# Moving half of a projection ahead of the last head's gather, and adding four strips in vector rows instead of a matrix product

## The chip, the cores and the metric

The kernel runs on one core of one Trainium2 chip. The metric is the device time of one execution in microseconds (us). Executions of one kernel agree to one or two tenths of a per cent (the six runs of before span 0.11%). All runs quoted were of the fast state. A ratio is the mean time of one kernel's fast runs over that of the other's of the same rounds, so it is not quite the ratio of the medians that are quoted.

In the profile, PE is TensorE's matmuls, PEld its weight loads, DVE is VectorE, ACT is ScalarE, SP the engine that issues the loads and stores. L733 is a line of the kernel's text; the changed kernels have other line numbers for the same code.

## The reference

Two attention blocks for one token: a large one, A (32 heads, 32,768 keys each), and a small one, B (32 query heads over 8 key heads, the last 4,096 keys). Each ends in a projection with its own `wo`.

```python
q = (x @ wq) per head
p = softmax(q @ k.T * Dh**-0.5)           # Dh = 128; B only over its last 4096 keys
o = p @ v                                  # 32 heads x 128
a = o_A.reshape(1, 32*128) @ wo_A          # [1, 512]
b = o_B.reshape(1, 32*128) @ wo_B          # [1, 512]
return concatenate([a, b], axis=-1)        # [1, 1, 1024], bf16
```

## The kernel before

The kernel streams keys and values of A head by head: TensorE transposes keys, VectorE copies the transposes out, TensorE forms scores and the value product. At the end of a head VectorE combines four diagonal blocks of the value product ("the combine") into `oc`, and TensorE puts the result into its row of a table G ("the gather"). After the last head G is normalised and spread over partitions, and the two projections follow.

```python
# end of emit_PV, the last step of each head
pv = self.emit_gather(name, g, DH, DH + 1)      # the softmax sum's column
for j in range(4):                               # VectorE: combine the four diagonal blocks
    ...
self.accread = o
self.gath = self.emit_gather(name, g, 0, DH)     # TensorE: the 128 values; waits for the combine
```

```python
def emit_proj(self):
    top = self.WO_CUTS["A"][1]                   # WO_CUTS: A (0,11,19,25,29,31,32), B (0,16,32)
    for part in range(len(self.WO_CUTS["B"]) - 1):        # small projection, four row strips of S
        o = self.proj_part("B", part, lambda e, lhsT, rhs, a: e.matmul(
            self.S[32 * (a % 4):32 * (a % 4) + 1, :], ..., tile_position=(0, 32 * (a % 4)), ...))
    strips = self.op("dve", ... tensor_copy(self.pb[:, :], self.S[:, :]), o)
    rows = o = self.op("pe", ... matmul(self.ACC[0:1, :], lhsT=self.e32[:, 0:1], rhs=self.pb[:, :]), strips, ...)
    o = self.op("dve", ... tensor_copy(self.qrow[0:1, :], self.ACC[0:1, :]), o)
    self.op("sp", ... dma_start(self.out[0, :, 512:1024], self.qrow[0:1, :]), o)
    row = self.proj_part("A", 0, ... self.T[1][0:1, :] ...)          # large projection, piece 1: 11 matmuls
    row = self.op("dve", ... tensor_copy(self.pb[0:1, :], self.T[1][0:1, :]), row, rows)  # "the T-row copy"
    for part in range(1, len(self.WO_CUTS["A"]) - 1):                # pieces 2 to 5, halves in PT
        if part == 3:
            self.op("pe", ... add the T-row to PT with a 1x1 matmul, row)
        self.proj_part("A", part, ...)
    ...                                          # piece 6, output copies, store
```

Each piece of a projection waits for its own load of `wo`. Each operation raises **one** semaphore, that of one reading engine (`to`). A second reading engine is kept in `pending`, and gets its signal from a **later** operation of the same engine that has a free signal:

```python
for o in ops:                                    # in assign(), for each engine's operations in order
    ...
    if to is None:
        to = next((c for c in users + pending), None)   # users: the engines that read this operation
    o.to = to
    pending = [c for c in dict.fromkeys(pending + users) if c != to]
```

That is correct as long as an engine's later operation ends after its earlier one, as in the trace of before (TensorE's small projection ends at 1312.92, the strip product at 1314.73, the first large piece at 1317.11), and every run here was correct. It says nothing about when. Engines are taken in the order PE, DVE, ACT, POOL, SP.

## Time and profile before

| | us |
|---|---|
| median of the first 3 runs (range) | 1323.32 (1322.72 to 1324.0) |
| span of the profiled run | 1321.7 |
| last data of `wo` landed (semaphore record in the trace) | 1318.82 |
| last matmul ends | 1320.02 |

From the page: the DMA row gives the busy share of the 16 DMA engines in 40 slices, in tenths.

```profile
DMA  9999999999999999999999999999999999999998
...
DMA packets 13359, 570.59 MB, mean 432 GB/s; under 512 B 1570, under 2 KB 1700, under 8 KB 2084
```

The load stream is full from end to end. The timeline of TensorE, in the middle of the loop and at the start of the last head (columns: start us, us, engine, line, operation, what it writes <- reads, count, and in brackets the idle time before it and what ended that):

```profile
661.72 3.49 PE L553 MATMUL psT<-ident,kbuf 128*128 128x128 bf16 x31 [4.82 <-DMA kbuf<-in_A_k_cache_dram]
...
1275.77 1.40 PE L553 MATMUL psT<-ident,kbuf 128*128 128x128 bf16 x22 [0.95 <-PEq L262]
```

In the middle of the loop TensorE waits 4.8 us for keys. In the last head, whose keys are there already, it waits only for its own sequencer at the end of the loop turn. The chain of waits at the end (start us, us, what):

```profile
1309.67 3.27 PE psS L733 x32
...
1312.97 0.70 DVE pb L736
...
1313.71 1.02 PE psACC L737 x2
1314.73 2.27 PE psT L741 x11
1317.01 3.02 PE psPT L719 x42
...
1320.05 0.41 DVE out_sb L726
```

The chain holds no load: the small projection (L733), strip copy, strip product (L737) and large projection (L741, L719) follow each other, and the last matmul ends 1.2 us after the last landing. The last view has busy time by stretches (us and instructions for each engine, then PEclk, the granted clock); the stretches are those on which the clock was granted:

```profile
core 0: us, PE busy (x) PEld busy (x) DVE busy (x) ACT busy (x) POOL busy (x), PEclk, DMA share, GB/s
1305.68:1309.09 3.41, 1.28 (x20) 0.54 (x12) 1.83 (x6) 0.00 (x0) 0.00 (x0) 1.00 0.99 421
1309.09:1312.50 3.41, 3.10 (x32) 1.11 (x36) 0.26 (x2) 0.00 (x0) 0.00 (x0) 0.50 0.98 415
1312.50:1315.90 3.40, 2.60 (x17) 0.70 (x10) 1.37 (x2) 0.00 (x0) 0.00 (x0) 1.00 1.00 419
```

The small projection fell into a stretch at half clock, the large one into stretches at full clock.

### The profile page before, as it was taken

Reading aid. Unit: us, or ns where it says so; the run is one execution under the profiler, and the core shown is the slowest. Engines: PE = TensorE matmul, PEld = TensorE weight load, DVE = VectorE, ACT = ScalarE, POOL = GpSimd, SP = SyncE. Lnnn points to the kernel's source line nnn. Section 1 sums busy time; section 2 is a strip of 40 time slices with the busy share of each in tenths; the row PEclk is TensorE's granted clock in tenths of the full one; section 3 lists DMA queues with packets and bytes.
Section 4 is the critical chain, followed back from the end, with each engine's and each line's share of the span. In section 5 each row is a group of like instructions: output and inputs, shape, how many; then the busy total and the mean of one; then the engine's idle time right before and its main releaser. Section 6 shows DMA issues by size and latency. Waiting matters only on the chain. (4 is left out here: it accounts for less than half of the span.)

```text
span 1321.7 us, 28783 instructions
## 1 busy us (share of the span) xinstructions
PE 968.2 (73%) x13243; PEld 673.7 (51%) x13243; DVE 750.7 (57%) x1341; ACT 55.1 (4%) x168; POOL 2.6 (0%) x22
## 2 busy tenths in 40 slices
PE   4675768777677878767787777678777667877787
PEld 3353446555444655544465544446554445555453
DVE  3563556664555666455566645556665456665563
ACT  0000000000000000000000000000000000000000
POOL 0000000000000000000000000000000000000000
PEclk9886788887878888787888878888887788888788
DMA  9999999999999999999999999999999999999998
GB/s 404 434 434 431 440 434 434 434 436 432 433 436 436 428 438 434 428 438 434 428 442 430 428 442 432 430 438 434 437 432 432 438 430 434 438 428 436 436 428 365
DMA packets 13359, 570.59 MB, mean 432 GB/s; under 512 B 1570, under 2 KB 1700, under 8 KB 2084
## 3 DMA queue, kind: packets, MB, share of 16 engines
q1 hardware_dynamic: 13060, 570.43, 99.8%
q8 instruction: 8, 0.13, 0.0%
q10 hardware_dynamic: 288, 0.00, 0.0%
q14 instruction: 3, 0.02, 0.0%
HBM read 570.43 MB, written 0.00 MB: 432 GB/s over the span
## 5 line engine op out<-in xcount | busy, mean ns | idle before, releaser
L557 DVE COPY kt<-psT 128x1024 bf16<-128x1024 bf16 x1056 | 654.3, 683 | 236.9 <-PE psT L553 235.5
L553 PE MATMUL psT<-ident,kbuf 128*128 128x128 bf16 x8448 | 577.8, 234 | 169.0 <-DMA kbuf<-in_A_k_cache_dram 154.4
L553 PEld LDWEIGHTS psT<-ident,kbuf 128*128 128x128 bf16 x8448 | 538.1, 106 | 261.2 <-DMA kbuf<-in_A_k_cache_dram 162.5
L656 PE MATMUL psACC<-vbuf,ptsb 128*4 128x512 bf16 (+1 forms) x2112 | 187.0, 531 | 22.8 <-ACT ptsb L631 22.0
L576 PE MATMUL psS<-kt,qw 128*32 128x512 bf16 x2048 | 157.7, 385 | 14.9 <-DVE kt L557 14.9
L670 DVE TENSOR_SCALAR oc_A<-psACC,hot_A 128x128 f32<-128x128 f32 x32 | 11.2, 350 | 251.9 <-PE psG L683 251.9
L656 PEld LDWEIGHTS psACC<-vbuf,ptsb 128*4 128x4 bf16 (+1 forms) x2112 | 59.8, 111 | 140.4 <-issue 93.1
L604 ACT ACTIVATE psb<-psS,nb_A 128x512 bf16<-128x512 f32 x32 | 22.0, 687 | 1166.5 <-DVE nb_A L603 1166.5
L576 PEld LDWEIGHTS psS<-kt,qw 128*32 128x32 bf16 x2048 | 34.0, 95 | 57.6 <-DVE kt L557 30.8
L683 PE MATMUL psG<-oc_A,hw 128*32 128x128 f32 (+1 forms) x128 | 19.3, 227 | 52.3 <-DVE oc_A L672 52.3
L683 PEld LDWEIGHTS psG<-oc_A,hw 128*32 128x32 f32 x128 | 11.4, 109 | 62.4 <-DVE oc_A L672 55.0
L628 PE MATMUL psPT<-ident,psb 128*128 128x128 bf16 x136 | 18.3, 279 | 34.0 <-ACT psb L604 34.0
L672 DVE SCALAR_TENSOR_TENSOR oc_A<-psACC,hot_A,oc_A 128x128 f32<-128x128 f32 x96 | 33.6, 350 | 3.4
L593 DVE TENSOR_REDUCE tr_in<-psS 128x1 f32<-128x512 f32 x34 | 23.5, 692 | 17.2 <-PE psS L576 17.2
L628 PEld LDWEIGHTS psPT<-ident,psb 128*128 128x128 bf16 x136 | 10.3, 119 | 37.1 <-ACT psb L604 36.7
L597 PE MATMUL psACC<-rows,tr_in 128*1 128x64 f32 x64 | 8.7, 217 | 25.6 <-DVE tr_in L593 25.6
L631 ACT ACTIVATE ptsb<-psPT 128x512 bf16<-128x512 bf16 x34 | 20.3, 597 | 30.9 <-PE psPT L628 30.9
L597 PEld LDWEIGHTS psACC<-rows,tr_in 128*1 128x1 f32 x64 | 2.7, 81 | 35.1 <-DVE tr_in L593 35.1
L601 PE MATMUL psACC<-mr_A,nscale 1*128 1x1 f32 x64 | 12.1, 256 | 9.8 <-DVE mr_A L600 9.8
L601 PEld LDWEIGHTS psACC<-mr_A,nscale 1*128 1x128 f32 x64 | 9.4, 182 | 15.8 <-DVE mr_A L600 15.8
L603 DVE COPY nb_A<-psACC 128x1 f32<-128x1 f32 x32 | 5.0, 157 | 15.1 <-PE psACC L601 15.1
L600 DVE TENSOR_REDUCE mr_A<-psACC 1x1 f32<-1x64 f32 x32 | 6.8, 213 | 11.7 <-PE psACC L597 11.7
(82 smaller groups left out, 74.9 us busy)
## 6 DMA issues: line engine op xcount, KB each, us to landing
kbuf<-in_A_k_cache_dram SPq DMA_DIRECT2D x4, 4096.0 KB, 23.2
kbuf<-in_B_k_cache_dram SPq DMA_DIRECT2D x2, 4096.0 KB, 31.6
vbuf<-in_B_v_cache_dram SPq DMA_DIRECT2D x2, 4096.0 KB, 25.4
vbuf<-in_B_wq_dram SPq DMA_DIRECT2D x1, 4096.0 KB, 12.4
vbuf<-in_A_wq_dram SPq DMA_DIRECT2D x1, 4096.0 KB, 31.9
kbuf<-in_B_wo_dram SPq DMA_DIRECT2D x2, 2048.0 KB, 33.1
kbuf<-in_A_wo_dram SPq DMA_DIRECT2D x1, 1408.0 KB, 27.4
kbuf<-in_A_wo_dram SPq DMA_DIRECT2D x1, 1024.0 KB, 29.5
```

Source lines behind the costliest of these rows:

```text
L553: inst = e.transpose(T[:, 128 * k:128 * k + 128], src[:, DH * k:DH * k + DH], self.ident[:, :])
L557: self.copies.append(self.op("dve", lambda v: v.tensor_copy(KT[:, :], T[:, :]), o, to="pe"))
L576: inst = e.matmul(self.S[32 * c:32 * c + 32, :], lhsT=win, rhs=self.kt[(bb + c // 2) % NKT][:, 512 * (c % 2):512 * (c % 2) + 512], start=b ...
L593: o = dve(lambda v: v.reduce_max(tr["in"][:, 0:1], self.S[:, :], axis=AXX), self.sdone, self.k_pool, to="pe" if name == "A" else None)
L597: o = self.op("pe", lambda e: e.matmul(self.ACC[0:1, 0:64], lhsT=tr["in"][:, 0:1], rhs=self.rows64[:, :], start=True, stop=True, skip_grou ...
L601: o = self.op("pe", lambda e: e.matmul(self.ACC[:, 64:65], lhsT=self.nscale[:, :], rhs=t["mr"][0:1, :], start=True, stop=True, skip_group_ ...
L604: self.sread = self.op("act", lambda s: s.activation(out=self.psb[:, :], in_=self.S[:, :], func=ACTF.Exp, bias=t["nb"][:, k:k + 1], scale= ...
L628: inst = e.transpose(PT[:, 128 * jj:128 * jj + 128], self.psb[:, 128 * jj:128 * jj + 128], self.ident[:, :])
L631: self.ptread = self.op("act", lambda s: s.activation(out=self.ptsb[:, :], in_=PT[:, 0:512], func=ACTF.Copy), self.psread, to="pe")
L656: inst = e.matmul(acc[32 * c:32 * c + rows, 0:512], lhsT=lhsT, rhs=rhs, start=begin, stop=end, tile_position=(0, 32 * c), skip_group_check ...
L672: o = self.op("dve", lambda v, src=src, hot=hot: v.scalar_tensor_tensor(out=oc, in0=src, scalar=hot, in1=oc, op0=ALU.mult, op1=ALU.add), p ...
L683: return self.op("pe", lambda e: e.matmul(self.G[0:32, c0 + c:c0 + c2], lhsT=win, rhs=t["oc"][g % len(t["oc"])][:, c:c2], start=False, sto ...
```

## The change

The intent is to shorten TensorE's tail. Half of the small projection is put ahead of the last head's gather, to run while VectorE combines. For that the gather of each head moves to the start of the next loop turn, and the last one stands after the loop. The four strips are added in rows on one partition by ScalarE (two copies) and VectorE (one copy, three adds), so the strip copy and the fp32 product leave TensorE's path. A few clears are moved or added.

```diff
@@ the loop and what follows it
             self.emit_qcopy(g)
+            self.gath = self.emit_gather("A", g - 1, 0, DH)
             self.emit_unit("A", g)
 ...
+        self.emit_proj_b(0)
+        self.gath = self.emit_gather("A", NQH - 1, 0, DH)
         self.emit_spread("A")
         self.emit_proj()
@@ end of emit_PV
-        self.gath = self.emit_gather(name, g, 0, DH)
+        if name == "B":
+            self.gath = self.emit_gather(name, g, 0, DH)
@@
+    def sum_strips(self, o):
+        S = [self.S[32 * c:32 * c + 1, :] for c in range(STRIPS)]
+        row = [self.kt[c][0:1, :].bitcast(F32) for c in range(STRIPS)]
+        act = lambda c: self.op("act", lambda e: e.activation(out=row[c], in_=S[c], func=ACTF.Copy), o)
+        add = lambda out, a, b, *deps: dve(lambda v: v.tensor_tensor(out=out, in0=a, in1=b, op=ALU.add), *deps)
+        one, three = act(1), act(3)
+        two = dve(lambda v: v.tensor_copy(row[2], S[2]), o)
+        x = add(row[0], S[0], row[1], o, one)
+        y = add(row[2], row[2], row[3], two, three)
+        return add(self.qrow[0:1, :], row[0], row[2], x, y)
@@ emit_proj
-        for part in range(len(self.WO_CUTS["B"]) - 1):
-            o = self.proj_part("B", part, ...)
-        strips = self.op("dve", ... tensor_copy(self.pb[:, :], self.S[:, :]), o)
-        rows = o = self.op("pe", ... matmul(self.ACC[0:1, :], lhsT=self.e32[:, 0:1], rhs=self.pb[:, :], ...), strips, ...)
-        o = self.op("dve", ... tensor_copy(self.qrow[0:1, :], self.ACC[0:1, :]), o)
+        o = self.emit_proj_b(1)
+        o = self.sum_strips(o)
 (cut: the clears, the zero gather of the first turn, pb cut to one row)
```

More of the change, by code (lines that the diff above doesn't have):

```diff
@@ L284, in alloc @@
         self.m4 = sb("m4", [1, 128], F32)
-        self.pb = sb("pb", [128, 512], F32)
+        self.pb = sb("pb", [1, 512], F32)
         self.out_sb = sb("out_sb", [1, 512], BF16)
@@ L456, in constants @@
             pattern=[[-32, 4], [-1, 16]], compare_op=ALU.is_equal, fill=0.0, base=0, channel_multiplier=1), rows)
+        pool(lambda g: g.memset(c["A"]["oc"][0][:, :], 0.0))
+        self.k_hw = pool(lambda g: g.memset(self.hw[:, :], 0.0))
         pool(lambda g: g.memset(self.nscale[:, :], -self.SCALE))
@@ L460, in constants @@
             self.k_pool = pool(lambda g, n=n: g.memset(c[n]["b"][:, :], 0.0))
-        self.k_hw = pool(lambda g: g.memset(self.hw[:, :], 0.0))
         dve = lambda fn, *deps, **k: self.op("dve", fn, *deps, **k)
@@ L684, in emit_gather @@
             self.G[0:32, c0 + c:c0 + c2], lhsT=win, rhs=t["oc"][g % len(t["oc"])][:, c:c2], start=False, stop=True,
-            skip_group_check=True), self.accread, self.sread, self.hcopy if name == "A" else self.k_sel, to="dve")
+            skip_group_check=True), *(self.accread, self.sread, self.hcopy if name == "A" else self.k_sel) if g >= 0 else
+            (self.k_hw, self.accread), to="dve")
     def emit_spread(self, name):
@@ L727, in store, with emit_proj_b @@
         return self.op("act", lambda e: e.activation(out=out, in_=src, func=ACTF.Copy), dep)
+    def emit_proj_b(self, part):
+        return self.proj_part("B", part, lambda e, lhsT, rhs, a: e.matmul(
+            self.S[32 * (a % 4):32 * (a % 4) + 1, :], lhsT=lhsT, rhs=rhs, start=(a < 4), stop=(a >= 28),
+            tile_position=(0, 32 * (a % 4)), skip_group_check=True))
+    def sum_strips(self, o):
+        S = [self.S[32 * c:32 * c + 1, :] for c in range(STRIPS)]
+        row = [self.kt[c][0:1, :].bitcast(F32) for c in range(STRIPS)]
+        dve = lambda fn, *deps: self.op("dve", fn, *deps)
+        act = lambda c: self.op("act", lambda e: e.activation(out=row[c], in_=S[c], func=ACTF.Copy), o)
[5 more added lines that the diff above has]
+        return add(self.qrow[0:1, :], row[0], row[2], x, y)
     def emit_proj(self):
         top = self.WO_CUTS["A"][1]
-        for part in range(len(self.WO_CUTS["B"]) - 1):
-            o = self.proj_part("B", part, lambda e, lhsT, rhs, a: e.matmul(
-                self.S[32 * (a % 4):32 * (a % 4) + 1, :], lhsT=lhsT, rhs=rhs, start=(a < 4), stop=(a >= 28),
-                tile_position=(0, 32 * (a % 4)), skip_group_check=True))
-        strips = self.op("dve", lambda v: v.tensor_copy(self.pb[:, :], self.S[:, :]), o)
-        rows = o = self.op("pe", lambda e: e.matmul(self.ACC[0:1, :], lhsT=self.e32[:, 0:1], rhs=self.pb[:, :], start=True,
-                                             stop=True, skip_group_check=True), strips, self.accread)
-        o = self.op("dve", lambda v: v.tensor_copy(self.qrow[0:1, :], self.ACC[0:1, :]), o)
+        o = self.emit_proj_b(1)
+        o = self.sum_strips(o)
         self.op("sp", lambda e: e.dma_start(self.out[0, :, 512:1024], self.qrow[0:1, :]).then_inc(self.outsem["B"], 16), o)
@@ L742, in emit_proj @@
             self.T[1][0:1, :], lhsT=lhsT, rhs=rhs, start=(a == 0), stop=(a == top - 1), skip_group_check=True))
-        row = self.op("dve", lambda v: v.tensor_copy(self.pb[0:1, :], self.T[1][0:1, :]), row, rows)
+        row = self.op("dve", lambda v: v.tensor_copy(self.pb[:, :], self.T[1][0:1, :]), row)
         for part in range(1, len(self.WO_CUTS["A"]) - 1):
             if part == 3:
-                self.op("pe", lambda e: self.halves(e, self.PT, self.e32[0:1, 0:1], self.pb[0:1, :], False, False), row)
+                self.op("pe", lambda e: self.halves(e, self.PT, self.e32[0:1, 0:1], self.pb[:, :], False, False), row)
             self.proj_part("A", part, lambda e, lhsT, rhs, a: self.halves(e, self.PT, lhsT, rhs, a == top, False)
```

## The prediction

> **What bounds the kernel now.** The load stream. The page's DMA row shows 9 tenths in all but the last slice: 570.59 MB at 432 GB/s. In the trace's packets the stream starts 2 us into the span, has no pause, and its last data packet ends near 1318.3 of 1321.7 us. In the loop the timeline shows TensorE 4.8 us idle per head (at 661.72, for instance) until keys land, while each value load is issued some 8 us before the key load ahead of it is through. [...] So nothing that TensorE saves inside the loop can count; only the tail can.
>
> **The tail before** (timeline, chain of waits). The last value product ends about 1306.35; VectorE combine 1306.62 to 1308.14; gather 0.42; normalise and spread to 1309.6; small projection 3.27 (32 matmuls); strip copy on VectorE 0.70; fp32 strip product 1.02 (TensorE stands 0.74 for the copy, about 0.86 for the product); the large projection, 1314.6 to 1320.03, back to back; out copies 0.41; store. The large block's six wo pieces have landed (semaphore records) at 1312.28, 1314.75, 1316.65, 1317.87, 1318.48, 1318.82. TensorE is 1.2 us behind the loads at the end.
>
> **What the change does.**
> - In each loop turn the gather moves past the loop branch, so the 0.95 us of sequencer time before the transposes (at 1275.77 a wait on PEq) runs under VectorE's 1.5 us combine. 31 turns have this swallowed by the wait for keys; only the last head, which starts without waiting for a load, keeps it: about 0.9 us.
> - Half of the small projection (1.65 us) goes under the last combine. The loop exit now stands ahead of it, so about 0.8 us is real.
> - Strip copy and product leave TensorE: 1.6 us. In their place two ScalarE rows, one VectorE copy and three VectorE adds, about 0.68 us each (estimate from 1x512 copies at 0.679 and 128x512 ScalarE copies at 0.60 to 0.69): some 2.8 us instead of 2.5 to the small result, off the path; VectorE is free before the T-row copy is wanted.
> - A gather of zeros in the first turn, a small memset: nothing.
>
> Sum on TensorE: about 3.3 us. But it then meets the loads. After the last landing, 1318.82, 4 short matmuls remain (0.3 to 0.4 us), against an end at 1320.03 now. So I expect 0.8 to 0.9 us of the 3.3 in the time; the rest becomes TensorE waiting for wo pieces.
>
> **Prediction: 1322.5 us**, 1321.0 to 1324.2 for 8 in 10 (the three runs before spread over 1.3 us, more than the gain). Faster by over 2%: 0.4%; within 2%: 99%; slower: 0.6%.
>
> **What would show it.** Loop: same 432 GB/s, waits for keys about 0.9 us longer per head. Last head's transposes about 0.9 us earlier. Tail: 16 small matmuls between the last value product and the gather; TensorE waits for wo before the large pieces; last matmul ending 0.3 to 0.4 us after the last landing; the chain of waits ending in a DMA landing.
>
> **What would make it wrong.** The granted clock flips between 0.5 and 1.0 in steps of 3.41 us (0.5 from 1309.09 to 1312.5). With more waiting in the tail, 0.5 could be granted during the large projection; 11 matmuls of 0.21 us would take 0.43 and the tail end up to 2 us later than now (I give 10%). [...] Or the sum on VectorE delays the T-row copy.

0.9, 0.8 and 1.6 us make the 3.3 us on TensorE, of which 0.8 to 0.9 us were expected in the time.

## The result, and the profile after

Measured: 1325.45 us median (1325.02 to 1327.86, 6 runs), against 1322.84 (1322.54 to 1324.0, 6 runs) for before in the same comparison. The ratio is 1.0023, with a 95% interval of 1.001 to 1.0036: a small loss, clear of noise, where a small gain had been predicted. The measured median lies above the predicted range.

The page of the kernel after, the same lines:

```profile
DMA  9999999999999999999999999999999999999997
...
DMA packets 13360, 570.59 MB, mean 431 GB/s; under 512 B 1571, under 2 KB 1701, under 8 KB 2085
```

The stream is the same, and so are the landings: the last data of `wo` had landed at 1318.89 (1318.82 before). The timeline answers the two lines shown of before, and adds the two halves of the small projection:

```profile
661.77 3.49 PE L557 MATMUL psT<-ident,kbuf 128*128 128x128 bf16 x31 [4.81 <-DMA kbuf<-in_A_k_cache_dram]
...
1274.81 2.41 PE L557 MATMUL psT<-ident,kbuf 128*128 128x128 bf16 x40
...
1304.36 1.03 PE L737 MATMUL psS<-kbuf,oz_B 128*1 128x512 bf16 x13
...
1309.06 1.85 PE L737 MATMUL psS<-kbuf,oz_B 128*1 128x512 bf16 x16 [1.62 <-DMA kbuf<-in_B_wo_dram]
```

The loop is unchanged, the last head starts 0.96 us earlier, and half of the small projection does run ahead of the gather. TensorE now waits for loads already at the small block's second piece. So far this is the plan. The chain of waits shows what came after:

```profile
1312.41 4.17 PE psT L760 x11
1316.58 1.00 PE psPT L725 x10
...
1317.60 0.60 ACT kt L746
...
1318.22 0.69 DVE kt L747
...
1318.91 0.69 DVE kt L747
...
1319.63 0.68 DVE qrow L747
1320.31 0.61 DVE pb L762
...
1320.96 1.46 PE psPT L725 x17
...
1322.45 0.41 DVE out_sb L732
```

It reads as follows. The small projection was done near 1310.9. ScalarE copies its first strip (`kt L746`) only at 1317.60, at once after TensorE's work on `psPT`, which belongs to the *large* projection. VectorE's three adds follow, then the T-row copy (`pb L762`), and only then can TensorE add the T-row and finish. The waits (engine, line and what it waited for: us in total, times, longest) say the same:

```profile
ACT kt L746 <- PE psPT L725: 18.5, 1, 18.5
...
DVE kt L747 <- ACT kt L746: 6.6, 1, 6.6
...
PE psPT L725 <- DVE pb L762: 2.8, 1, 2.8
```

The stretches by granted clock show a second difference: the first piece of the large projection (L760, 11 matmuls) ran mostly at half clock: 4.17 us on the chain of waits, where before took 2.27 us at full clock.

```profile
1305.71:1309.13 3.42, 0.74 (x10) 0.37 (x14) 1.04 (x4) 0.00 (x0) 0.00 (x0) 1.00 1.00 428
1309.13:1312.54 3.41, 1.90 (x17) 0.41 (x18) 0.69 (x1) 0.00 (x0) 0.00 (x0) 0.50 0.97 413
1312.54:1315.96 3.42, 3.42 (x10) 1.01 (x9) 0.00 (x0) 0.00 (x0) 0.00 (x0) 0.50 0.99 413
```

### The profile page after: what moved, and what is told of

Read it like the earlier page. It is cut to its first block, busy times and chain, and to the rows that moved or that the text cites. A ratio compares the mean times of both kernels' runs of the same rounds, so it can differ in the third digit from the quotient of the medians.

```text
span 1324.1 us, 28790 instructions
## 1 busy us (share of the span) xinstructions
PE 969.3 (73%) x13243; PEld 674.8 (51%) x13243; DVE 752.5 (57%) x1343; ACT 56.4 (4%) x170; POOL 2.8 (0%) x23
## 4 chain that ended last, share of the span: by engine, by line
DMA 70%; PE 28%; DVE 2%; issue 0%; ACT 0%; SPq 0%
DMA kbuf<-in_A_k_cache_dram 65%; PE psT L557 23%; PE psS L580 4%; DMA kbuf<-in_B_k_cache_dram 3%; DMA kbuf<-in_A_wo_dram 2%; DVE kt L561 1%; PE psACC L660 0%; PE psT L760 0%; PE psPT L725 0%; DVE kt L747 0%; DVE oc_A L676 0%; PE psPT L632 0%; ACT psb L608 0%; DVE tr_in L597 0%; DVE qrow L747 0%
```

## The experiments

Two theories came out of the trace, and they are not exclusive. **S (late signal):** the last small matmul has two reading engines. Its one signal goes to VectorE. ScalarE's is left pending; the next operation, piece 1 of the large projection, spends its signal on VectorE too (for the T-row copy), and piece 2 is the first with a free one. So ScalarE waits for 27 large matmul steps (11, and 16 halves), and the T-row copy stands behind it in VectorE's order. **K or C (clock):** the waits that the change put into TensorE's tail cost it the full clock, and the half clock costs the time. The clock is granted in stretches of 3.41 us (1309.09 to 1312.50 in before, for instance), and where their boundaries lie differs from trace to trace; the texts call this the clock's grid. Rivals: the sum is simply too much work for VectorE and ScalarE (V), or the two moves lose by themselves (M).

Every run was correct, and each kernel was timed in five rounds against before on the same chip. Idle matmuls, or fillers, are matmuls whose result nobody reads.

| kernel | edit | median (range), us | before there, median | ratio (95%) |
|---|---|---|---|---|
| after again | none | 1325.86 (1324.86 to 1326.28) | 1322.63 | 1.0024 (1.0011 to 1.0038) |
| x1_signal | after + own signals | 1323.33 (1322.52 to 1323.56) | 1322.73 | 1.0 (0.9986 to 1.0014) |
| x2_dve | after, sum on VectorE only | 1323.53 (1322.4 to 1323.69) | 1322.73 | 1.0002 (0.9988 to 1.0015) |
| x3_warm | after + 4 idle matmuls | 1324.84 (1323.75 to 1325.88) | 1322.73 | 1.0014 (1.0 to 1.0028) |
| x4_oldsum | after with the old sum | 1323.3 (1322.44 to 1323.58) | 1322.73 | 1.0002 (0.9988 to 1.0015) |
| x6_rowfirst | after, T-row copy first | 1323.74 (1322.82 to 1324.28) | 1322.63 | 1.0008 (0.9995 to 1.0022) |
| x7_signal_warm | after + own signals + 6 idle matmuls | 1322.37 (1322.2 to 1322.42) | 1322.63 | 0.9997 (0.9983 to 1.0011) |
| x8_before_warm | before + 4 idle matmuls per head | 1322.47 (1322.19 to 1322.72) | 1322.63 | 0.9997 (0.9984 to 1.0011) |
| x5_sumonly | before + new sum | 1324.05 (1323.84 to 1324.91) | 1322.51 | 1.0013 (0.9999 to 1.0026) |
| x9_before_sum_signal | before + new sum + own signals | 1322.11 (1322.0 to 1322.42) | 1322.51 | 0.9996 (0.9982 to 1.001) |

### x1_signal: each reader its own signal

```diff
-        o = self.emit_proj_b(1)
-        o = self.sum_strips(o)
+        even = self.op("pe", some([*range(16, 29), 30]), (self.wosem["B"][1], 16), self.c["B"]["ozop"], to="dve")
+        odd = self.op("pe", some([29, 31]), to="act")      # some(seq): the same small matmuls, in this order
+        o = self.sum_strips(even, odd)                      # ScalarE's two copies depend on odd, the rest on even
```

> The changed kernel, with only this different: the last four small matmuls run in the order of strips 0, 2, then 1, 3, and the first pair signals VectorE, the second ScalarE (before, one signal went to VectorE alone and ScalarE's came with a later TensorE step). Theory S (late signal): ScalarE's two row copies start within 0.2 us of the last small matmul (about 1311) instead of at 1317.60; the three adds end before 1315; the T-row copy starts right after the 11th large matmul; the last matmul ends 0.3 to 0.4 us after the last wo landing; time 1322.4 (1321.9 to 1322.9), 3 us below the changed kernel and 0 to 0.9 below before. Rival C (half clock in the large projection, 3.84 us for 11 matmuls, costs the time): no change, 1325 or more, as nothing touches the clock. Rival V (three adds and copies on VectorE and ScalarE are simply too long): no change either, as the same seven instructions run.

Measured: 1323.33 us, 2.1 us below the change's first median (other rounds). ScalarE starts at 1310.21, right after the last small matmul:

```profile
1310.21 1.20 ACT L746 ACTIVATE kt<-psS 1x512 f32<-1x512 f32 x2 [11.30 <-PE psS L761]
...
1312.45 4.00 PE L770 MATMUL psT<-kbuf,oz_A 128*1 128x512 bf16 x9 [2.32 <-DMA kbuf<-in_A_wo_dram]
...
1320.50 0.41 DVE L732 CAST out_sb<-psPT 1x256 bf16<-1x256 f32 x1 [2.48 <-PE psPT L725]
```

What follows: S is right about most of the loss. The same copies and adds ran, so V falls; the half clock was still there (9 of the first 11 large matmuls take 4.00 us), so C alone falls. But the range was missed: the runs make two groups, 1322.5 to 1322.6 and 1323.3 to 1323.6. In this trace the last matmul ended at 1320.47, 1.5 us after the last landing (1318.94), at half clock until 1317.70. The stretches:

```profile
1307.46:1310.87 3.41, 1.29 (x20) 0.45 (x20) 1.37 (x4) 0.64 (x2) 0.00 (x0) 1.00 0.99 424
1310.87:1314.28 3.41, 1.83 (x5) 0.59 (x6) 2.00 (x3) 0.54 (x1) 0.00 (x0) 0.50 1.00 423
```

### x2_dve: no ScalarE in the sum

```diff
-        one, three = act(1), act(3)
-        two = dve(lambda v: v.tensor_copy(row[2], S[2]), o)
-        x = add(row[0], S[0], row[1], o, one)
-        y = add(row[2], row[2], row[3], two, three)
-        return add(self.qrow[0:1, :], row[0], row[2], x, y)
+        x = dve(lambda v: v.tensor_copy(row[0], S[0]), o)
+        x = add(row[1], S[1], row[0], x)
+        x = add(row[2], S[2], row[1], x)
+        return add(self.qrow[0:1, :], S[3], row[2], x)
```

> The changed kernel, with the four strips added by VectorE alone (one copy, three adds that read a strip in PSUM each), no ScalarE. Theory S: the only reader is VectorE, which gets its signal at once; four steps of about 0.68 us from 1310.9, done near 1313.7; time 1322.4 (1321.9 to 1322.9). Rival C (half clock): 1325 or more. Rival V (VectorE work too long): VectorE has as many full steps of the sum as before the experiment (four), so no change, 1325.

Measured: 1323.53 us, with one run at 1322.4 and four from 1323.1 to 1323.7. It agrees with x1_signal by another way: VectorE's four steps ran from 1309.92 to 1312.76, and TensorE did not wait for the T-row. The clock was again at 0.5 (here from 1311.32 to 1318.15), and 9 of the first 11 large matmuls took 4.00 us as in x1. The loss goes when the second reader goes; what is left over goes with neither.

### x3_warm: keep the clock, leave the late signal

```diff
+        def fill(e):                              # ahead of piece 1 of the large projection
+            for a in range(4):
+                inst = e.matmul(self.T[2][0:1, :], lhsT=ozb[:, a:a + 1], rhs=wob[:, 512 * a:512 * a + 512],
+                                start=True, stop=True, ...)       # into an unused bank, read by nobody
+            return inst
+        self.op("pe", fill, to="pe")
```

> The changed kernel, with four idle matmuls into an unused bank between the small and the large projection, so that TensorE is busy while it waits for the first large wo piece. The late signal stays. Expected clock: 1.0 instead of 0.5 from about 1312.5, and 11 large matmuls in 2.4 us instead of 3.84. Theory S: ScalarE's signal comes with the end of the second large piece, now near 1315.9 instead of 1317.5, so ScalarE starts 1.6 us earlier, and so does all that follows: time 1323.8 (1323.3 to 1324.2), and the slow third of the runs (1327.7) goes away. Rival C: the whole loss goes, time 1322.5 or less.

Measured: 1324.84 us; two runs at 1323.8 as S expected, two at 1324.8 and one at 1325.9. The median misses both forecasts. The trace is of one of the better runs:

```profile
1312.39 2.54 PE L767 MATMUL psT<-kbuf,oz_A 128*1 128x512 bf16 x11 [1.42 <-DMA kbuf<-in_A_wo_dram]
...
1315.92 1.21 ACT L746 ACTIVATE kt<-psS 1x512 f32<-1x512 f32 x2 [16.61 <-PE psPT L725]
...
1319.29 0.59 PE L725 MATMUL psPT<-pb,e 1*1 1x256 f32 x4 [1.72 <-DVE pb L769]
```

At full clock the first large piece takes 2.54 us, piece 2 ends at 1315.88, and ScalarE starts 0.04 us later, as forecast: its start follows piece 2. TensorE still waits 1.72 us for the T-row. So the clock is a part of the loss, since it moves piece 2, but not the whole. The slower three runs have no trace; that four fillers are too few in some positions of the clock's grid is likely and not shown.

### x4_oldsum: the two moves without the new sum

```diff
-        o = self.sum_strips(o)
+        strips = ...; rows = o = ...; o = ...     # the strip copy, fp32 product and row copy of the kernel before
```

> The changed kernel, with the old strip sum (VectorE copy of 128x512, fp32 TensorE product, VectorE row copy); the gather and half of the small projection stay where the change has put them. Theory S: the loss was all in the new sum, so the two moves show what they are worth alone: small projection ends near 1310.9, strip copy 1311.7, product 1312.6, large projection from 1312.6, last matmul bound by the last landing near 1318.9; time 1322.4 (1321.9 to 1322.9). Rival M (the moves themselves lose, by letting TensorE stand at the wo pieces): 1325. Rival C: the product keeps TensorE busy, so it would fall here too; this run does not tell S from C, the other three do.

Measured: 1323.3 us, again two groups (1322.4 to 1322.5, and 1323.3 to 1323.6). The moves do not lose what the change lost, so M falls as the cause of the loss. They do not gain either. The clock was at half again when the product ran: it took 1.87 us against 1.02 in before, and 9 of the first 11 large matmuls 2.93 us against 2.10. That the product keeps TensorE's clock up, as rival C had it, was not shown. In the trace, a run of the better group, the last matmul ended at 1319.09, 0.31 us after the last landing (1318.78). The expected median of 1322.4 was reached by two runs of five.

### after_again: the change unedited

> The changed kernel once more, unedited, so that its spread and a second trace stand beside the next three on one chip. Theory S (late signal) with K (the clock's 3.41 us grid lies differently from run to run): 1325.0 to 1327.9 again, median near 1325.5; in the trace ScalarE's first row copy starts within 0.1 us of the end of the second large piece (the 27th large matmul step), wherever the clock has put that, and the T-row copy 2.6 to 2.7 us after it. A rival in which ScalarE is held by something else would break that tie.

Measured: 1325.86 us (1324.86 to 1326.28), one run just below the forecast.

```profile
1316.96 1.20 ACT L746 ACTIVATE kt<-psS 1x512 f32<-1x512 f32 x2 [17.78 <-PE psPT L725]
```

In this second trace piece 2 of the large projection ends between 1316.82 and 1316.91 and ScalarE starts at 1316.96; in the first trace piece 2 ends between 1317.45 and 1317.55 and ScalarE starts at 1317.60. (The trace does not number the halves of a piece. The earlier figure of each pair counts 16 halves by their start, the later one eight of the half that lags behind.) The T-row copy started 2.6 us after ScalarE in both (1319.59 and 1320.24). The clock's grid lay 2.3 us later here, and 9 of the first 11 large matmuls took 3.39 us instead of 3.84. The two runs at 1327.7 and 1327.9 of the first comparison did not come again, and no trace has them.

### x6_rowfirst: T-row copy ahead of the sum in VectorE's order

```diff
         o = self.emit_proj_b(1)
-        o = self.sum_strips(o)
-        self.op("sp", ... store of the small result, o)
         row = self.proj_part("A", 0, ...)
         row = self.op("dve", ... tensor_copy(self.pb[:, :], self.T[1][0:1, :]), row)
+        o = self.sum_strips(o)
+        self.op("sp", ... store of the small result, o)
```

> The changed kernel, with the T-row copy put ahead of the strip sum in VectorE's order, nothing else; ScalarE's signal stays late. Theory S (late signal reaches the path only through VectorE's order, because the T-row copy stands behind an add that waits for ScalarE): ScalarE still starts late (1315.9 to 1317.7), but TensorE no longer waits for the T-row, and the last matmul ends at 1319.1 to 1320.5 according to the clock; the small store goes out near 1318.7 to 1320.4, no later than the large one by more than 0.5 us: time 1322.4 to 1323.7, median about 1323.2. If ScalarE's lateness hurt directly (by its own output copy or by the small store), the time would stay above 1324.5.

Measured: 1323.74 us (1322.82 to 1324.28); the median and the two slower runs lie above the forecast's upper end, and have no trace. The trace is of the fastest run:

```profile
1316.22 0.68 DVE L760 COPY pb<-psT 1x512 f32<-1x512 f32 x1 [7.38 <-PE psT L758]
...
1317.10 1.20 ACT L746 ACTIVATE kt<-psS 1x512 f32<-1x512 f32 x2 [17.74 <-PE psPT L725]
1317.64 0.59 PE L725 MATMUL psPT<-pb,e 1*1 1x256 f32 x4
```

ScalarE is as late as ever (1317.10), but TensorE does not wait: it adds the T-row at 1317.64, and its last matmul ends at 1319.09. The order on VectorE is therefore the way by which the late signal reached the path. A second, smaller way is seen too: VectorE, still busy with the last add, copies its half of the output at 1319.73 instead of about 1319.1.

### x7_signal_warm: own signals and the clock kept

The edit is x1_signal with six of x3_warm's idle matmuls.

> The own-signal kernel (first experiment of this kind: 1322.5 to 1323.6 in two groups) plus six idle matmuls between the small and the large projection. Theory K (what the first repair still lacks is the clock at 0.5 during the large projection, 4.0 us and more for the first large piece, in runs whose grid lies badly): granted clock 1.0 through the large projection, the last matmul ends 0.3 to 0.4 us after the last wo landing in every run: 1322.4 median, all five within 1322.2 to 1322.9. If the two groups come from the load stream instead, they stay, with a median of 1323.3.

Measured: 1322.37 us, all five runs within 1322.20 and 1322.42, as forecast. The two groups are gone. The edit leaves the loads alone, so the load stream falls as their cause, and the clock fits; none of x1's better runs has a trace that would show it directly.

```profile
1309.86 1.46 PE L773 MATMUL psT<-kbuf,oz_B 128*1 128x512 bf16 x6
...
1312.35 2.54 PE L777 MATMUL psT<-kbuf,oz_A 128*1 128x512 bf16 x11 [1.04 <-DMA kbuf<-in_A_wo_dram]
...
1317.95 1.20 PE L725 MATMUL psPT<-kbuf,oz_A 128*1 128x256 bf16 x14
```

The last matmul ends at 1319.15, 0.32 us after the last landing at 1318.83. The stretch in which the fillers begin had TensorE busy for 2.07 of 3.42 us and the clock stayed at 1.0:

```profile
1307.02:1310.44 3.42, 2.07 (x25) 0.88 (x26) 1.06 (x4) 0.33 (x1) 0.00 (x0) 1.00 0.98 419
```

### x8_before_warm: before, with the clock kept

```diff
         self.accread = o
+        if name == "A":
+            ...                                   # four idle matmuls into T[2], while VectorE combines
         self.gath = self.emit_gather(name, g, 0, DH)
```

> The kernel before, with four idle matmuls while TensorE waits for VectorE's combine at the end of each head, nothing of the change. Theory K: in before, the runs at 1323.1 to 1323.8 are those in which the small projection runs at clock 0.5 (3.27 us instead of about 1.7), and those at 1322.4 to 1322.7 are already bound by the last landing. With the clock held up the small projection takes 1.7 us and every run is at the floor: 1322.4 median, all within 1322.1 to 1322.9. Then the change has nothing to gain over before in a good run. If the floor were elsewhere, this run stays at 1322.4 to 1323.8.

Measured: 1322.47 us, all within 1322.19 and 1322.72, as forecast.

```profile
1309.69 1.90 PE L740 MATMUL psS<-kbuf,oz_B 128*1 128x512 bf16 x32
...
1318.10 1.18 PE L726 MATMUL psPT<-kbuf,oz_A 128*1 128x256 bf16 x14
```

The small projection takes 1.90 us instead of 3.31, TensorE catches up with the loads, and the last matmul ends at 1319.28, 0.32 us after the last landing (1318.96). Without any part of the change, before reaches the same end. The clock's grid lies nearly where it lay in before's trace (a boundary at 1309.20, there at 1309.09), so the stretch ahead of the small projection can be compared: 2.16 us of TensorE time instead of 1.28, and the clock stayed at 1.0.

```profile
1305.79:1309.20 3.41, 2.16 (x24) 0.74 (x16) 1.83 (x6) 0.00 (x0) 0.00 (x0) 1.00 0.98 420
```

The times alone say less: seven of before's nine runs in these rounds, 1322.37 to 1322.70, lie in the same range. None of them has a trace, so that they too end with the last landing is likely and not shown.

### x5_sumonly: the new sum alone

The edit puts `sum_strips` into before, in place of the strip copy and product; gather and small projection stay.

> The kernel before with only the new strip sum (rows on ScalarE, adds on VectorE), gather and small projection where they were. Theory S (late signal): ScalarE again starts with the end of the second large piece, here 1315.9 to 1316.4, the T-row copy ends 3.3 us later, TensorE waits for it, and the last matmul ends at 1320.7 to 1321.2 against 1320.03: time 1323.7 to 1325.0, median 1324.1, slower than before by 1 to 1.5 us though it takes 1.6 us off TensorE. If the sum is harmless without the two moves, 1322.4 to 1323.3.

Measured: 1324.05 us (1323.84 to 1324.91), as S forecast: slower than before, though 1.6 us of TensorE's wait and product are gone. The interval of the ratio just reaches 1 (0.9999), but every run lies above every one of before's nine (1322.39 to 1323.36).

```profile
1316.15 1.21 ACT L734 ACTIVATE kt<-psS 1x512 f32<-1x512 f32 x2 [15.98 <-PE psPT L719]
...
1319.51 0.59 PE L719 MATMUL psPT<-pb,e 1*1 1x256 f32 x4 [1.72 <-DVE pb L753]
```

The clock was 1.0 throughout this tail, so here the late signal is alone, and TensorE waits 1.72 us for the T-row.

### x9_before_sum_signal: the new sum with own signals, in before

The edit is x5_sumonly with x1_signal's reordering.

> The same as the other kernel of this call, with the last four small matmuls reordered so that VectorE and ScalarE get their own signals. Theory S: ScalarE starts within 0.2 us of the last small matmul. Theory K (clock): the small projection still runs back to back from the last gather to near 1312.9 at the worst, so TensorE has little idle time ahead of the large projection, which starts at the first landing (1312.3 to 1312.9) at clock 1.0 and catches up with the loads: 1322.4 median, at most one run of five above 1322.9. If K is wrong and the runs split in two groups as those with the moves did, the median is 1323.3.

Measured: 1322.11 us, all within 1322.00 and 1322.42, as forecast.

```profile
1310.93 1.20 ACT L734 ACTIVATE kt<-psS 1x512 f32<-1x512 f32 x2 [10.77 <-PE psS L753]
...
1312.14 2.54 PE L762 MATMUL psT<-kbuf,oz_A 128*1 128x512 bf16 x11 [1.28 <-DMA kbuf<-in_A_wo_dram]
```

The small projection runs in one piece to 1310.85, 1.3 us before the large one starts, and in this trace the clock stays at 1.0 with no filler; the other four runs have none. The last matmul ends at 1318.94, 0.31 us after the last landing. This is the fastest kernel. It is 0.4 us below before's median of the same rounds; the interval of the ratio contains 1, so no more is claimed than that four of its five runs lie below all nine of before, and that its spread is smaller. Nor is the sum shown to be what put it ahead of x7: in this trace the last landing itself came 0.2 us earlier (1318.63 against 1318.83).

## Why the prediction was wrong

**What held.** The load stream bounds the kernel: it moved 432 GB/s before and 431 after, and the last landing moved by 0.07 us. The last head started 0.96 us earlier (0.9 predicted). The small gather of zeros cost nothing that shows. (The value loads are issued mostly 6 to 7.6 us ahead of the landing of the keys before them, not "some 8"; nothing rests on it.) With the loss repaired, the last matmul came 0.31 to 0.32 us after the last landing (x7, x9), where 0.3 to 0.4 had been predicted. That the loop gains nothing held as well, but the sign given for it did not: waits for keys do not get longer by 0.9 us (4.82 and 4.81 us). The loop branch had been inside that wait before, too.

**The step that failed** is "off the path; VectorE is free before the T-row copy is wanted". The sum was costed rightly (three adds of 0.68 us each, ScalarE copies of about 0.6) but started at the wrong time: ScalarE was taken to start with the end of the small projection, near 1310.9, and it started at 1317.60. The prediction looked at what each new operation reads, and not at which signal would release it. With two engines reading one TensorE result and one signal to give, ScalarE was released by piece 2 of the large projection. VectorE, which ran its operations in the program's order, held the T-row copy from 1316.7, when the T-row was ready, to 1320.24, and TensorE stood 2.75 us; with the copy first in that order (x6) it ran at 1316.22. "The sum on VectorE delays the T-row copy" was listed among the risks, but without cause or odds. x1, x2 and x6 each remove this wait by a different way; x5 makes it in before. Counted from the last landing, the last matmul ended 3.53 us later in the change's first trace, 1.53 with own signals (x1) and 0.32 with own signals and fillers (x7): about 2.0 us for the late signal and 1.2 for the clock.

**A term that was mis-sized** is the clock. The prediction gave one chance in ten that the large projection would be granted half clock. In all six traces that have the moves and no fillers (after, after_again, x1, x2, x4, x6) it was for one or two stretches: 9 of the first 11 large matmuls took 3.84, 3.39, 4.00, 4.00, 2.93 and 3.46 us, against 2.10 in before at full clock. It costs up to 1.3 us when the signal is repaired (last matmul at 1320.47 in x1, 1319.15 in x7). The number of half-clock stretches goes with the two groups: two in the traced runs of x1 and x2 (1323.56 and 1323.53 us, last matmul 1.53 and 1.90 us after the last landing), one in those of x4 and x6 (1322.44 and 1322.82 us, 0.31 and 0.32 us). The half clock also feeds the late signal by moving piece 2 (its end lies near 1317.5 in the change's first trace, at 1315.88 in x3 at full clock). The grants change in steps of 3.41 us, and the grid can lie at another place from run to run (a boundary at 1309.13 in the change's first trace, at 1311.44 in its second). What goes with a change of the clock in these traces is how long TensorE was busy in the stretch before: 1.28 us (before), 1.29 us (x1) and 0.74 us (after) of 3.41 were followed by half clock, 2.07 us (x7) were not; at half clock 1.90 us (after) did not win the full clock back and 3.10 us (before) did. The longest gap between matmuls inside the stretch that lost the clock was 1.64 us in before and 0.79 us in x1. Counted over the 375 stretches that each trace of before and after has from its first half clock (39.3 us) on, full clock was lost after 0 to 1.76 us of TensorE time and kept after 1.63 to 3.41; half clock stayed after 0 to 2.73 us and ended after 2.69 to 3.41. Busy times are as the profile models them. The change put TensorE's work up against the loads, which fits: with six matmuls whose result nobody reads (x7) the clock did not fall.

**The gain that was expected had no room.** The prediction compared with a traced run whose last matmul ended 1.2 us after the last landing. That run, at 1323.36, was one of before's poorer ones. The better ones, at 1322.4 to 1322.7, have no trace, but they lie at the level of x7 and x8, whose traces end with the last landing. Repaired only in its signal, the change's median is 1323.3, no better than before. Of its three parts only the new sum may have some worth, and only with its own signals (x9, whose interval contains 1). The prediction also listed the landings of the large block's `wo` alone. The small block's second piece landed at 1308.97 before and at 1309.01 after, and TensorE waited 1.62 us for it in the change's first trace: that much of what was saved ahead of it became waiting at once. The loop-exit cost ahead of the early half (estimate: of 1.65 us only about 0.8 real) was not seen either: those matmuls started in the same 0.1 us as the last gather column (1304.31).

**Still open:** the change's two runs at 1327.7 and 1327.9, the slower runs of x3 and the slower ones of x6. They fit a less lucky clock grid, but have no trace.

## What to carry to other kernels

When work moves from one engine to two, look up which instruction will signal each of them, and what stands behind them in their queues: a reader that is signalled late is as slow as one that works late (here ScalarE, at 1317.60 instead of near 1310.9), and an engine that runs its operations in the program's order passes its wait on to work that has nothing to do with it (here the T-row copy, for which TensorE stood 2.75 us). When a kernel ends with its loads, as this one does, time saved on an engine can turn into waiting (here 1.62 us for the small block's second piece), and that waiting can cost TensorE its clock for the work that must still follow (here up to 1.3 us, in x1 against x7). Before claiming a tenth of a per cent, find out whether the traced run of before is one of its good ones.
